# Two decoder layers in fp32 from one stream of loads: new order and places at the turn, w1 in seven groups, halves of exp

## The chip, the cores and the metric

The kernel runs on one core of a Trainium2 chip. The metric is the device time of one execution in microseconds. Everything is fp32.

## The reference

Two layers of decoding for 8 sequences, one token each. Each layer is attention over a cache of 4096 positions (32 query heads in 4 groups) and then a dense network of width 3584. Both layers use the same weights and the same caches.

```
def _A_ref(x, k_cache, v_cache, wq, wo):
    q = (x @ wq).reshape(B, Sq, Hq, Dh).transpose(0, 2, 1, 3)
    k = jnp.repeat(k_cache, rep, axis=1)
    v = jnp.repeat(v_cache, rep, axis=1)
    scores = jnp.einsum("bhqd,bhkd->bhqk", q, k) * (Dh ** -0.5)
    p = _softmax(scores, axis=-1)
    o = jnp.einsum("bhqk,bhkd->bhqd", p, v)
    return o.transpose(0, 2, 1, 3).reshape(B, Sq, Hq * Dh) @ wo

def _B_ref(x, w1, b1, w2, b2):
    h = _gelu(jnp.einsum("bsd,df->bsf", x, w1) + b1)
    return jnp.einsum("bsf,fd->bsd", h, w2) + b2

x = x + _A_ref(_layernorm(x), ...)
x = x + _B_ref(_layernorm(x), ...)
x = x + _A_ref(_layernorm(x), ...)
x = x + _B_ref(_layernorm(x), ...)
```

B = 8, D = 1024, Hq * Dh = 4096, F = 3584. Each cache is 64 MiB, wq and wo are 16 MiB each, w1 and w2 14 MiB each.

## The kernel before

**Memory.** Nearly all of SBUF is one tile, `arena`, of 52 units. A unit is 1024 columns of fp32 on 128 partitions, 512 KiB. A piece of K or V (one of 4 groups of heads, one half of the positions) is 1 MiB, two units; a batch has 8 pieces of K and 8 of V. All loads stand in one list, `stream`, in the order in which they are wanted: key, number of units, source and possible first units. `pump` (L214) takes from its head as long as the head's units are free, and issues the load on SP's queue. `release` (L226) frees a slot and pumps again. The queue is in order: a load that waits for its units holds all behind it. The order of PE's work is the order in which the program is written.

**Layer 0.** wq fills units 0 to 28 and goes on lying there through layer 0's attention, for layer 1 (`park`, L604, moves the rest of it aside). Units 48 to 52 hold the rows of scores and the turned probabilities (`arena.own`). Units 28 to 48 are a ring: `around` (L628) lists the caches' loads so that each begins where the last one ended, with at most 8 units in a load. For each batch `attention` (L572) goes through 8 pieces of K (`scores`, L479), then `probs` (L500: maximum over the positions, exp), `turn` (L512: eight transposes into `S`, two copies, and the total of exp by a matmul) and 8 pieces of V (`values`, L531). The result of each pair of V pieces is folded by DVE (L541, L543) and turned into a column of `oT` by `heads` (L548), one V piece later. In the last batch, 7, six pieces of K stay in units 36 to 48: layer 1 goes through the batches backwards and uses them first.

**Dense part of layer 0.** From the turn of batch 7 on, three blocks of 4 units, 28, 32 and 48, take wo (8 loads) and w1 (7 loads) in rotation. `expand` (L240) has w1 in three groups of 2048, 1024 and 512 columns (`GROUPS`). At the end of a group DVE takes it out (L264); at the next `flush` `hidden_unit` (L318) turns it, adds b1 and makes the gelu, into `hT`.

**The turn, `swap` (L382).** w2 comes in 4 columns of 28 tiles. Each column is three loads: a small one, "u", of 4 tiles (1 unit) that is given up after use, and 16 and 8 tiles (4 and 2 units) that stay for layer 1. For each column c PE does w2's products, DVE copies (L403), PE turns the result into x (L407), and then come the products of two tiles of wq (L417) with this new x, for the next layer's q. These free wq's units, into which the next columns of w2 and layer 1's first K and V are loaded. The small piece of column c+1 is used in `transient`, which is called between column c's copy and its turning, so ahead of column c's wq products. With the last column come the layernorm's moments and the square root (L465).

**Layer 1.** Attention over batches 7 to 0 in a ring over units 16 to 28 and 36 to 48, with at most 12 units in a load. Then wo in three loads (8, 12, 12 units), w1 in 12 and 4, 4 and 4, and 2, 1, 1 units, and the 4 small pieces of w2, the rest of which lies in the arena. `begin` runs w2's products for tiles 4 to 16 after the first half of w1's second group; the others come behind w1.

## Time and profile before

| | us |
|---|---|
| median of 3 runs | 899.94 (898.69 to 906.64) |
| the profiled execution | 903.69 |
| its span | 901.9 |
| PE busy | 556.9 |
| the load queue's packets, share of 16 DMA engines' span | 94.2% |
| read from HBM | 358.83 MB |

The span runs from the first to the last instruction of the program in one profiled execution; a run's time has some 1.8 us beside it. A page of the profile has each engine's busy time, the chain of waits that ended last, and groups of instructions by line (L488 is line 488 of the kernel) with what they waited for. PE is the matmul engine, PEld its weight loads, DVE and ACT the vector and the activation engine, SP the queue that issues loads. An fp32 matmul is two records. PEclk is the share of PE's full clock that was granted.

### The profile page before, as it was taken

To read this page: it belongs to the slowest core of one execution; us is meant where nothing else is said; L and a number is where in the kernel's file an instruction comes from. 1 tells how busy PE (TensorE), PEld (TensorE's weight loads), DVE (VectorE), ACT (ScalarE), POOL (GpSimd) and SP (SyncE) were. 2 spreads that over 40 slices of the span, in tenths; PEclk is the share of its full clock that TensorE was granted. 3 is DMA by queue.
4 is the path that set the end of the run, shared out by engine and by line. 5 is a ranking of instruction groups with operands and counts; after the bars stand their busy time and mean duration, and the time that the engine had idled before them with its cause. 6 is when DMAs were issued, how large, how long until landed. Compare 5 with 4: busy or idle time off the path is not lost.

```text
span 901.9 us, 9145 instructions
## 1 busy us (share of the span) xinstructions
PE 556.9 (62%) x4034; PEld 193.9 (22%) x4034; DVE 189.5 (21%) x616; ACT 50.1 (6%) x78; POOL 1.9 (0%) x12
## 2 busy tenths in 40 slices
PE   0767566665767576556568665666647567464477
PEld 0212122121212112222223221121202112122234
DVE  0013131212213131201211331322303122130011
ACT  0110000000000000000001100000000000000000
POOL 0000000000000000000000000000000000000000
PEclk9967778768667785878788986878868777787789
DMA  9999999999999998999996979999999999999990
GB/s 400 421 440 417 431 392 433 429 390 419 397 438 412 427 427 315 379 428 429 405 382 239 404 317 427 420 413 435 430 426 430 423 418 433 429 428 428 419 406 11
DMA packets 17895, 359.54 MB, mean 399 GB/s; under 512 B 1984, under 2 KB 2368, under 8 KB 3648
## 3 DMA queue, kind: packets, MB, share of 16 engines
q1 hardware_dynamic: 17712, 358.82, 94.2%
q8 instruction: 31, 0.51, 0.2%
q10 hardware_dynamic: 144, 0.15, 0.0%
q14 instruction: 8, 0.07, 0.0%
HBM read 358.83 MB, written 0.13 MB: 398 GB/s over the span
## 4 chain that ended last, share of the span: by engine, by line
DMA 48%; PE 37%; DVE 8%; ACT 3%; issue 2%; another core or an unknown queue 1%; SPq 0%; ACTq 0%; DVEq 0%
DMA arena<-in_k_dram 25%; PE sps L488 13%; PE o_ps L538 8%; DMA arena<-in_w_dram 7%; DMA arena<-in_wo_dram 6%; DMA arena<-in_v_dram 5%; DMA arena<-in_wq_dram 5%; PE sps L519 3%; PE acc L254 2%; ACT arena L509 2%; DVE arena L493 2%; PE y L371 2%; PE y L341 2%; PE acc L292 2%; PE sps L371 1%
## 5 line engine op out<-in xcount | busy, mean ns | idle before, releaser
L488 PE MATMUL sps<-arena,qz 128*32 128x512 f32 x1024 | 167.2, 805 | 118.1 <-DMA arena<-in_k_dram 109.5
L538 PE MATMUL o_ps<-arena 128*32 128x512 f32 x1024 | 162.5, 762 | 11.1 <-DMA arena<-in_v_dram 11.1
L488 PEld LDWEIGHTS sps<-arena,qz 128*32 128x32 f32 x1024 | 38.9, 139 | 242.1 <-issue 130.2
L493 DVE TENSOR_SCALAR_CACHE_REDUCE arena<-sps 128x512 f32<-128x512 f32 x32 | 22.1, 692 | 248.1 <-PE sps L488 248.1
L543 DVE SCALAR_TENSOR_TENSOR scr<-o_ps,bits,scr 128x128 f32<-128x128 f32 x192 | 67.4, 351 | 6.8
L341 PE MATMUL y<-arena,oxT 128*32 128x256 f32 x512 | 40.9, 481 | 39.8 <-DMA arena<-in_wo_dram 39.8
L519 PE MATMUL sps<-ident,arena 128*128 128x128 f32 x128 | 31.4, 391 | 38.6 <-DVE oxT L551 22.5
L538 PEld LDWEIGHTS o_ps<-arena 128*32 128x32 f32 x1024 | 31.4, 131 | 78.0 <-issue 62.4
L509 ACT ACTIVATE arena<-arena,bits 128x1024 f32<-128x1024 f32 x16 | 18.4, 1148 | 535.4 <-DVE scr L506 535.4
L254 PE MATMUL acc<-arena,oxT 128*32 128x512 f32 (+1 forms) x288 | 34.7, 616 | 17.0 <-DMA arena<-in_w_dram 16.4
L550 PE MATMUL sps<-bits,scr 128*128 128x8 f32 x128 | 25.8, 274 | 31.0 <-DVE scr L543 25.5
L541 DVE TENSOR_SCALAR scr<-o_ps,bits 128x128 f32<-128x128 f32 x64 | 22.5, 351 | 96.1 <-PE o_ps L538 96.1
L550 PEld LDWEIGHTS sps<-bits,scr 128*128 128x128 f32 x128 | 20.0, 197 | 86.3 <-DVE scr L543 73.6
L292 PE MATMUL acc<-arena,oxT 128*32 128x512 f32 (+1 forms) x250 | 34.4, 662 | 4.6 <-DMA arena<-in_wq_dram 4.3
L341 PEld LDWEIGHTS y<-arena,oxT 128*32 128x32 f32 x512 | 18.7, 134 | 61.6 <-DMA arena<-in_wo_dram 39.1
L519 PEld LDWEIGHTS sps<-ident,arena 128*128 128x128 f32 x128 | 20.2, 195 | 45.0 <-ACT arena L509 28.9
L371 PE MATMUL sps<-arena,oxT 128*32 128x256 f32 x224 | 17.8, 444 | 9.8 <-DMA arena<-in_w_dram 8.7
L502 PE MATMUL sps<-scr,bits 128*128 128x128 f32 x32 | 8.1, 337 | 21.3 <-DVE scr L498 21.3
L525 DVE COPY arena<-sps 128x512 f32<-128x512 f32 x16 | 11.1, 692 | 44.5 <-PE sps L519 44.5
L551 DVE TENSOR_TENSOR oxT<-sps,scr 128x8 f32<-128x8 f32 x64 | 11.0, 171 | 40.5 <-PE sps L550 40.5
L254 PEld LDWEIGHTS acc<-arena,oxT 128*32 128x32 f32 x288 | 11.0, 127 | 36.1 <-issue 18.9
L188 PE MATMUL sps<-ident,xb 128*128 128x128 f32 x12 | 3.1, 351 | 24.4 <-DMA xb<-in_x_dram 23.2
(106 smaller groups left out, 200.9 us busy)
## 6 DMA issues: line engine op xcount, KB each, us to landing
arena<-in_v_dram SPq DMA_DIRECT2D x16, 4096.0 KB, 17.6
arena<-in_k_dram SPq DMA_DIRECT2D x15, 4096.0 KB, 15.5
arena<-in_k_dram SPq DMA_DIRECT2D x16, 2048.0 KB, 16.7
arena<-in_v_dram SPq DMA_DIRECT2D x15, 2048.0 KB, 15.9
arena<-in_k_dram SPq DMA_DIRECT2D x5, 6144.0 KB, 18.6
arena<-in_v_dram SPq DMA_DIRECT2D x5, 6144.0 KB, 25.4
arena<-in_w_dram SPq DMA_DIRECT2D x14, 2048.0 KB, 12.5
arena<-in_wo_dram SPq DMA_DIRECT2D x8, 2048.0 KB, 11.5
```

Source lines behind the costliest of these rows:

```text
L254: nc.tensor.matmul(out_j, xnT[:, kt * XS:kt * XS + 32], src, start=(j not in begun), stop=(kt >= NT - (4 if split else 1)))
L292: nc.tensor.matmul(acc[u][32 * j:32 * j + 32, d0 - j * CH:d1 - j * CH], xnT[:, kt * XS:kt * XS + 32], ap[:, d0 - c0:d1 - c0], start=(kt == ...
L341: nc.tensor.matmul(y[32 * j:32 * j + 32, 0:Q4], lhs[:, n * B:n * B + 32], slot.ap[:, c + j * Q4:c + (j + 1) * Q4], start=(n == 0), stop=(n ...
L371: nc.tensor.matmul(y[32 * g:32 * g + 32], hT[:, kt * B:kt * B + 32], w2_at[c, kt], start=first, stop=(kt >= NFT - 4 if j is None else kt = ...
L488: nc.tensor.matmul(ps[32 * g:32 * g + 32, :], qz[:, c:c + 32], kt[:, g * CH:(g + 1) * CH], start=(j == 0), stop=(j == HKV - 1))
L493: nc.vector.tensor_scalar(st["row", b].ap[:, half * CH:(half + 1) * CH], ps, SCALE, None, op0=ALU.mult, op1=ALU.max, accum_out=st["mx", b] ...
L509: nc.scalar.activation(row, row, AF.Exp, bias=bias, scale=1.0, accum_out=ls)
L519: nc.tensor.transpose(pp[:, t * P:(t + 1) * P], row[:, c:c + P], ident)
L538: nc.tensor.matmul(o[32 * g:32 * g + 32, :], s[:, g], v[:, g * CH:(g + 1) * CH], start=(half == 0), stop=(half == NH - 1))
L541: nc.vector.tensor_scalar(r, o[:, 0:P], sel_t[:, 0:1], None, op0=ALU.mult)
L543: nc.vector.scalar_tensor_tensor(r, o[:, t * P:(t + 1) * P], sel_t[:, t:t + 1], r, op0=ALU.mult, op1=ALU.add)
L550: nc.tensor.matmul(po[:, 0:REP], r_s[j % 2], sel_h, start=True, stop=True)
```

## The change

In words:

- `swap`: `transient` is gone. Each column's three pieces of w2 are multiplied together, in the order `W2_ORDER` (the small one first or last), and the column's small piece is released there. The places of w2's loads are new.
- w1 is laid out in seven groups of 512 columns, each one block of 4 units. `expand` flushes ahead of each group. In layer 1 `grow` multiplies the w2 tiles of group u after w1's products of group u + 1.
- exp runs in two halves, each with its own total. `turn` transposes both halves, into two PSUM banks; DVE copies the first, ACT the second. The total's matmul is a new function, `totals`, after the second V piece. The second half of the scores has the bank `pt`.
- `heads` runs two tiles later than before, in the next batch if need be.
- Six pieces of batch 7's V are kept in place of six of its K.
- The ring functions are gone; each load's place is listed. wo in layer 1 comes in 4, 12, 8, 4, 2, 2 units, w1 in blocks of 4, the last one 2 and 2.
- `warm` runs a tanh right behind each square root.
- `bias_row` (the row of b2) is made during attention of layer 1 and added after the layernorm; in layer 0 it stays after w1's first group.

The diff, cut:

```diff
+W2_KTS = {"u": range(4), 0: range(4, 20), 1: range(20, NFT)}
+W2_ORDER = ("u", 0, 1), (0, 1, "u"), (0, 1, "u"), ("u", 0, 1)
+G = CH
+NGR = F // G
-GROUPS = 2048, 1024, 512
...
+    def warm():
+        nc.scalar.activation(sums["warm"], epst, AF.Tanh)
...
             nc.vector.reciprocal(rs, sd)
+            warm()
...
+        for u in range(NGR):
             acc = ps_o.tile([P, CH], F32, tag="o", name="acc")
+            kt = 0
+            flush()
             for i, slot in enumerate(tiles((name, u))):
+                for c in range(0, slot.cols, G):
+                    j = kt % 4
+                    nc.tensor.matmul(acc[32 * j:32 * j + 32, :], xnT[:, kt * XS:kt * XS + 32], slot.ap[:, c:c + G],
+                                     start=(kt < 4), stop=(kt >= NT - 4))
+                    kt += 1
                 release(slot)
                 flush()
+            if u in hooks:
+                hooks[u]()
+            nc.vector.tensor_scalar(row_s, acc, rs, None, op0=ALU.mult)
+            pending.append(lambda u=u: hidden_group(u, row_s))
...
+    def down_row(y, kts, cs=range(CB)):
         for kt in kts:
+            for c in cs:
+                nc.tensor.matmul(y[32 * c:32 * c + 32], hT[:, kt * B:kt * B + 32], w2_at[c, kt],
+                                 start=st["y0"][c], stop=(kt == NFT - 1))
...
     def swap():
+        flush()
         ys = small_ps("s")
-        transient(0)
-        flush()
...
         for c in range(CB):
-            for e, k0 in enumerate((UK, UK + 16)):
-                arrive(("w2", c, e), c, k0)
-            down(half(c), c, range(UK, NFT))
+            y = ys[:, c % 2 * Q4:(c % 2 + 1) * Q4]
+            kts = []
+            for kind in W2_ORDER[c]:
+                kts += arrive(c, kind)
+            down(y, c, kts)
+            release(held.pop(("w2u0", c)))
             ysb = row_s[:, c % 2 * Q4:(c % 2 + 1) * Q4]
-            nc.vector.tensor_copy(ysb, half(c))
-            if c + 1 < CB:
-                transient(c + 1)
+            nc.vector.tensor_copy(ysb, y)
...
-            st["ps", half] = small_ps("s")
+            st["ps", half] = small_ps(("s", "pt")[half])
...
-        nc.scalar.activation(row, row, AF.Exp, bias=bias, scale=1.0, accum_out=ls)
-        nc.vector.tensor_scalar(dl_s[b % 2], sel_x, ls, None, op0=ALU.mult)
+        for h in range(NH):
+            part = row[:, h * CH:(h + 1) * CH]
+            nc.scalar.activation(part, part, AF.Exp, bias=bias, scale=1.0, accum_out=ls[:, h:h + 1])
...
+    def turn(b):
...
+        for half in range(NH):
+            pp = small_ps(("pt", "s")[half])
...
+            if half == 0:
+                nc.vector.tensor_copy(dst, src)
+            else:
+                nc.scalar.activation(dst, src, AF.Copy)
...
+    def totals(b):
+        pl = small_ps("pt")
+        nc.tensor.matmul(pl[:, 0:HQ], ones, dl_s[b % 2], start=True, stop=True)
+        nc.vector.reciprocal(rl_s[b % 2], pl[:, 0:HQ])
+        st.pop(("row", b)).free()
...
+        def step():
+            for e in ready:
+                e[0] -= 1
+            while ready and ready[0][0] < 0:
+                heads(*ready.pop(0)[1:])
...
+                    if key[2:] == (0, NH - 1):
+                        totals(key[1])
+                step()
+                if key[0] == "v" and key[3] == NH - 1:
+                    ready.append([1, *key[1:3]])
...
-    kept = {("k", *k_at(last_b, r)) for r in range(n_kept)}
+    kept = {("v", *v_at(last_b, r)) for r in range(NR - n_kept, NR)}
...
+    cycle = [(((8, 32), (4, 40), (4, 44)), ((8, 28), (8, 36))), (((4, 44), (8, 28), (4, 36)), ((8, 40), (8, 28))),
+             (((8, 36), (4, 44), (4, 28)), ((8, 32), (8, 40))), (((8, 28), (4, 36), (4, 40)), ((4, 44), (8, 28), (4, 36))),
+             (((8, 40), (4, 28), (4, 32)), ((8, 36), (4, 44), (4, 28)))]
+    for n, b in enumerate(orders[0][:-1]):
+        batch(0, b, *cycle[n % 5])
+    batch(0, last_b, ((8, 36), (4, 44), (4, 28)), ((4, 32), (8, 36), (4, 44)))
...
+    for u in range(NGR):
+        weights(("i0", u), w1[0][:, u * NT * G:(u + 1) * NT * G], [4], blocks)
     i, j, k = LAST_BLOCKS
-    add(down_weights(0, ("u", 0, 1), 0), i + 3, j, i)
-    add(down_weights(1, ("u", 0, 1), 0), i + 2, k, i + 2)
-    add(down_weights(2, (0, 1, "u"), 0), 0, 4, 6)
-    add(down_weights(3, ("u", 0, 1), 0), 7, 8, 12)
+    down_weights(0, 0, i + 3, j, i)
+    down_weights(1, 0, k, i + 2, 0)
+    down_weights(2, 0, 2, 6, 1)
+    down_weights(3, 0, 0, 8, 12)
...
+    batch(1, last_b, ((4, 16), (4, 20), (4, 24), (4, 16)), ((4, 20),) if n_kept else ())
+    batch(1, last_b - 1, ((4, 24), (4, 16), (4, 20), (4, 36)), ((8, 40), (8, 16)))
...
+    weights(("o1",), wo[0], [4, 12, 8, 4, 2, 2], fixed(24, 36, 16, 24, 36, 38))
+    for u, (sizes, spots) in enumerate([([4], (at,)) for at in (40, 44, 16, 20, 24, 36)] + [([2, 2], (40, 42))]):
+        weights(("i1", u), w1[0][:, u * NT * G:(u + 1) * NT * G], sizes, fixed(*spots))
     for c in range(CB):
-        add(down_weights(c, ("u",), 1), 40 + c)
+        down_weights(c, 1, 44 + c)
...
+            groups = [range(GT * u, GT * (u + 1)) for u in range(NGR)]
+            expand("i1", rs, {u + 1: lambda u=u: grow(u) for u in range(1, NGR - 2)})
+            down_row(y[0], groups[NGR - 2][:2])
             flush()
+            down_row(y[0], groups[NGR - 2][2:])
             for c in range(CB):
+                arrive(c, "u")
+                down_row(y[0], groups[0], [c])
+            down_row(y[0], groups[NGR - 1])
             nc.vector.tensor_tensor(x_row, x_row, y[0], ALU.add)
```

The places in a pair such as (8, 32) are the number of units and the first unit; `LAST_BLOCKS` is now 28, 32, 48.

More of the change, by code (lines that the diff above doesn't have):

```diff
@@ L654, in lane, with cache @@
         return (layer, keys[0]), (kc if a == "k" else vc)[b][:, r * W:(r + m) * W]
-    def cache(layer, b, a, at, r=0):
+    def cache(layer, b, a, at):
+        r = 0
         while r < NR:
+            if layer == 1 and (a, *(k_at if a == "k" else v_at)(b, r)) in kept:
+                break
             n, starts = at(2 * (NR - r))
@@ L692, in decode_layers, with listed, batch @@
+    def listed(*spots):
+        spots = iter(spots)
+        return lambda left: next(spots)
+    def batch(layer, b, k_spots, v_spots):
+        for a, spots in (("k", k_spots), ("v", v_spots)):
+            stream.extend(cache(layer, b, a, listed(*((n, (at,)) for n, at in spots))))
     halves = lambda i: [[("q", kt, u) for kt in kts for u in range(2)] for kts in ((0, 1, 2, 3), (4, 5), (6,), ())][i]
     weights(("q0",), wq[0], [16, 8, 4, 4], fixed(0, 16, 24, 28), kept=halves)
-    ring = around(AREAS[0], 4, 8)
@@ L730, in decode_layers @@
         st["layer"] = layer
-        last = attention(orders[layer], kept if layer == 0 else (), {("turn", last_b): opened} if layer == 0 else {})
+        b2_row = spare[:, 0:Q4]
+        hooks = {("turn", last_b): opened} if layer == 0 else {
+            ("v", *v_at(last_b - 2, 0)): lambda: bias_row(b2_row, None, spare[:, Q4:Q4 + CH])}
+        last = attention(orders[layer], kept if layer == 0 else (), hooks)
         rsum = row_sums()
```

239 lines of the change are left out of this document (68 added, 171 removed).

## Prediction

> **What bounds the kernel now.** I read the page first, then a table of stretches with each stretch's granted clock and DMA rate, then the chain of waits inside the stretches that lose most.
>
> ```profile
> span 901.9 us, 9145 instructions
> ...
> PE 556.9 (62%) x4034; PEld 193.9 (22%) x4034; DVE 189.5 (21%) x616; ACT 50.1 (6%) x78; POOL 1.9 (0%) x12
> ...
> q1 hardware_dynamic: 17712, 358.82, 94.2%
> ```
>
> Then the stretches: start, end and length, busy time of each engine, granted clock, share of DMA time, GB/s.
>
> ```profile
> core 0: us, PE busy (x) PEld busy (x) DVE busy (x) ACT busy (x) POOL busy (x), PEclk, DMA share, GB/s
> 0.00:185.00 185.00, 104.88 (x646) 32.94 (x650) 35.13 (x112) 13.46 (x18) 1.57 (x11) 0.81 0.99 421
> 185.00:210.00 25.00, 18.29 (x108) 6.33 (x100) 7.73 (x26) 1.84 (x3) 0.00 (x0) 0.73 0.90 375
> 210.00:340.00 130.00, 83.17 (x484) 25.14 (x484) 31.59 (x102) 5.51 (x9) 0.00 (x0) 0.74 0.99 423
> 340.00:376.00 36.00, 22.64 (x120) 7.20 (x116) 9.14 (x30) 1.84 (x3) 0.00 (x0) 0.64 0.84 327
> 376.00:441.00 65.00, 37.58 (x394) 15.45 (x390) 5.12 (x15) 3.40 (x6) 0.00 (x0) 0.82 1.01 428
> 441.00:470.00 29.00, 20.40 (x208) 8.93 (x200) 5.01 (x19) 0.73 (x3) 0.31 (x1) 0.83 0.95 376
> 470.00:482.00 12.00, 7.49 (x41) 2.81 (x45) 0.17 (x1) 0.00 (x0) 0.00 (x0) 0.57 0.35 145
> 482.00:510.00 28.00, 23.87 (x255) 10.30 (x251) 8.30 (x27) 3.17 (x4) 0.00 (x0) 1.00 0.96 377
> 510.00:536.00 26.00, 17.92 (x118) 5.90 (x107) 9.06 (x29) 3.12 (x4) 0.00 (x0) 0.80 0.78 324
> 536.00:881.00 345.00, 204.96 (x1495) 70.41 (x1499) 74.23 (x240) 16.51 (x27) 0.00 (x0) 0.78 0.99 423
> 881.00:901.90 20.90, 15.75 (x202) 8.53 (x194) 4.00 (x15) 0.48 (x2) 0.00 (x0) 0.99 0.02 7
> ```
>
> One queue carries the loads and is busy 94.2% of the span; PE is busy 62%. So loads set the time wherever they run, and what can be won is the time in which they don't. The best long stretch (376 to 441) runs at 428 GB/s. I take that as the pace: 2 MiB (2.10 MB) is 4.90 us, the 512 KiB unit in which the kernel's places count 1.23 us. Each stretch loses its length times (1 - rate/428): 3.0 us to 185, 3.1 to 210, 1.5 to 340, 8.5 to 376, none to 441; then 3.5, 7.9, 3.3 and 6.3, together 21.0 us, to 536; 4.0 to 881. Behind the last load stand 20.9 us of PE work. The change doesn't alter the bytes: six kept pieces stay six, the kept part of w2 and wq stays the same. So the sum goes over three places: the turn between the layers (441 to 536), layer 0's last batch (340 to 376), and the tail.
>
> **The turn.** A row of the timeline (start, length; in brackets PE's idle time before it), then the longest pieces of the chain of waits behind it:
>
> ```profile
> 474.24 1.08 PE L371 MATMUL sps<-arena,oxT 128*32 128x256 f32 x8 [7.47 <-DMA arena<-in_w_dram]
> ```
>
> ```profile
> 477.18 5.82 PE acc L292 x30
> 482.99 2.85 PE sps L371 x45
> 488.20 3.44 PE acc L292 x30
> 491.64 2.83 PE sps L371 x45
> ```
>
> PE stands 7.47 us at 474 because the small w2 piece of column 2 (four tiles, `transient`) is queued on PE ahead of column 1's wq products, and it has not landed. Those wq products are what empties units 8 to 14 for column 3's loads, so the queue then stands too (145 GB/s in 470 to 482). The change puts each column's small piece into that column's own matmuls, behind the wq products of the column before; what PE waits for there is loaded before the places that those products empty. That hole goes.
>
> What is late next is the pace of a column itself. From 482.99 to 491.64 one column takes PE 8.65 us at clock 1.00: w2's matmuls, the copy, the turning, wq's products. It empties room for, and needs, seven units, 8.6 us of loads. These are as good as equal, so at full clock each of four columns may lose some tenths. The places agree: column 1's second piece (units 30, 31) waits for column 0's small piece to be read, which comes first in column 0's order; column 3's small piece (unit 0) waits for column 1's, the same way but last in its order, with three loads still ahead of it in SP's queue; columns 2 and 3 and the four K loads wait for wq products one column before their need. At half clock a column's wq products alone take 2.4 us more (5.82 against 3.44), w2's about as much: some 5 us a column. With no PE hole of several us I expect mostly full clock, as 482 to 510 had it. Column 0's large piece takes the place of the last w1 block but one, with 2.5 MiB queued in between instead of the 4 of three blocks in rotation: up to 2 us.
>
> All eight K pieces of batch 7 are now loaded instead of two, and its V is kept instead. This moves 6 MiB of loads ahead of the first scores in layer 1. They come through three blocks of 4 units that wq's last products empty, and are scored at 1.8 us a piece even near half clock (344.09 below: two pieces in 3.68) against 2.45 us of load, so PE keeps up; the V that is kept then needs no load, where in the trace of before the loads of 510 to 536 stood (324 GB/s) behind its values. I leave 3.5 us of the 21.0 (bounds 0 and 13: none, or half clock in two columns and a wait of 3 in the first batch). Gain 17.5 us.
>
> **Layer 0's last batch.** The longest pieces of the chain there:
>
> ```profile
> 344.09 3.68 PE sps L488 x16
> 347.80 0.71 DVE arena L493 x2
> 349.06 0.81 PE sps L502 x2
> 350.52 1.25 ACT arena L509 x2
> 352.26 1.10 PE sps L519 x4
> 354.03 1.13 PE sps L519 x4
> 355.18 0.70 DVE arena L525
> 356.57 5.32 PE o_ps L538 x24
> 361.91 7.75 DMA arena<-in_v_dram
> ```
>
> From the last score (347.77) to the first value take 8.8 us. K being kept in units 36 to 48, V has only units 28 to 36 until values free them, and comes in four loads of 1 MiB that each wait for values (361.91). With V kept, K's places 36 to 48 are free once scored, so all of V loads straight behind K, and two blocks of wo behind it into 28 and 32; the third needs 48 to 52, free when the last value is done. V's last load lands 9.8 us before the second wo block does, and V's last two pieces take PE 3.5 us at the rate of 356.57 (three in 5.32), so nothing stands. 8.5 us of loss become 1 (0 to 4). Gain 7.5.
>
> The shorter chain adds to that in each batch: halves of exp let the first four transposes start after 0.6 instead of 1.25 us, the second four go to another bank and no longer wait for the copy (0.67, from 353.36 to 354.03), and the copy's and the totals' time ahead of the first value (1.4, from 355.16 to 356.57) goes: some 2.5 us off 8.8. Heads, two tiles later, don't wait for DVE. A row of the waits: us in total, times, longest.
>
> ```profile
> PE sps L550 <- DVE scr L543: 25.5, 38, 0.8
> ```
>
> Under loads that are always running this is worth nothing; it counts where the ring stood, 185 to 210, where 3.1 us become 0.6: 2.5. The listed places walk through the same units in the same cyclic order as the old ring; only K's end now comes as a 2 MiB piece, so the last scores start with less to do. I count nothing for that, nor for the other stretches (3.0, 1.5, 4.0 stay). `warm` adds a table load of 1.28 us (874.37 below) on ACT behind each square root. At the turn the copy of q's second half is queued behind it, up to 1.3 us late (it lies in the turn's bounds); elsewhere ACT's next work comes some us later. The row of b2 for layer 1 is made in batch 5 of attention: two DVE products of 512 columns (0.67 each, as the eviction of 887.16 below) and the matmuls between, about 3 us of PE under running loads, so nothing, and 2 if the ring is full there. Layer 0's row of b2 now stands ahead of group 0's eviction and makes w1's first blocks 3 us late, within the 4.9 us that three blocks allow.
>
> **The tail.** The longest pieces of the chain, then one w1 block of layer 0 in the timeline.
>
> ```profile
> 874.37 1.28 ACT L329
> 876.44 5.39 PE y L371 x96
> 881.83 1.76 PE acc L254 x32
> 884.15 1.06 PE acc L254 x8
> 887.16 0.67 DVE scr L264
> 887.88 1.06 PE sps L273 x8
> 888.94 9.72 PE y L371 x128
> ```
>
> ```profile
> 416.31 1.92 PE L254 MATMUL acc<-arena,oxT 128*32 128x512 f32 x16 [1.18 <-DMA arena<-in_w_dram]
> ```
>
> Before, w1's first group is four blocks wide, so no w2 matmul can start until it is whole, turned and through tanh (876.44); by then loading is nearly over, and PE has all of w2 before it. After, a group is one block: 8 matmuls (1.92), four turning matmuls (1.06), and 16 w2 matmuls of the group before (a third of 5.39: 1.80), 4.8 us in all, beside 4.90 us of load; the eviction (0.67) lies beside the w2 matmuls. So at full clock PE is level with the loads. The last w1 block lands 4.9 us before the end of loading (2 MiB of small w2 pieces follow it). From there: 1.92, then the w2 matmuls of group 5 around the turning, about 3.1, which ends at the end of loading; then the small pieces and group 6's matmuls. 888.94 holds 64 matmuls; the first 32 at the rate of 876.44 are 3.6 us, so the other 32, the very ones that remain, 6.1. Then 3.2 us as now, from 898.66, where 888.94 ends, to the end of the span. 9.4 us; I take 10, bounds 9 and 15 (one block late). Gain 10.9.
>
> In the trace the clock is 0.99 in the busy tail and 0.57 in the stretch where PE stands; PE busy without gaps keeps it. [...]
>
> **Sum.** 17.5 + 7.5 + 2.5 + 10.9 = 38.4. 901.9 - 38.4 = 863.5 us of span. The profiled execution took 903.69, 1.8 more than its span, so 865.3 by its own measure; the median of the runs is 899.94, 3.75 below that execution. I predict 861.5.
>
> **Rivals.** *Half of the turn stays.* PE's column (8.65) against its loads (8.6) has no slack, and two columns at half clock, the first batch of layer 1 waiting for exp, and a tail at 15 give back 5 to 14: 867 to 877. For it: 470 to 482 ran at 0.57. Against: that clock followed PE's 7.47 us hole. 0.28.
>
> *A PE bound tail.* i1 at half clock throughout: 9.6 us a block against 4.9, five blocks late by 23, the end 6 longer: 891, within 1% of before. Against it: 0.99 in the tail of before. [...] 0.04.
>
> *The small pieces still hold the chain.* Units 30, 31 and 0 are reused by small pieces; if a hole of 8 us stays in another place, the time is 869. It lies inside the first rival and is counted there.
>
> *Slower.* The second half of the scores now shares a PSUM bank with heads, totals and the maximum's spread. If each batch's scores waited there until the ring's 10 MiB were full, every batch would stand. The gain of 38 is eaten at 2.6 us in each of 15 batches; 4 us in each give 921. For it: one such loss of 3.1 at 185 to 210. Against: heads run two tiles into the new batch, its bank is needed four tiles in. 0.05.
>
> **Numbers.** Forecast 0.59 (855 to 867), half the turn 0.28, tail 0.04, slower 0.05; 0.04 for better still: with none of the 10.6 us that I leave (3.5, 1, 0.6, 1.5, 4.0) and a tail of 9 it is 850. The range 849 to 879 leaves out somewhat over a tenth. One per cent, 9 us, is about what the runs (898.69 to 906.64) can tell from no change. Faster by more: 0.59 + 0.28 + 0.04 = 0.91; within: 0.04; slower: 0.05.
>
> **What would show it.** Right: no stretch of the turn under 350 GB/s, no PE wait over 3 us for a small w2 piece; no V load of 1 MiB in layer 0; w2 matmuls of layer 1 beginning some 22 us before loading ends, and 9 to 15 us between the last load and the end. Wrong: clock near 0.5 in the turn with wq products at 5.8 us, loads standing behind w2's places, or PE still at w1 blocks when the last load has landed.

## The result and the profile after

The changed kernel takes 863.33 us (median of 4 runs, 859.75 to 867.36) against 901.62 for the kernel before on the same chip (4 runs, 898.69 to 906.64). The ratio is 0.957, with a 95% interval of 0.951 to 0.964. 861.5 was predicted, with a range of 849 to 879. The profiled execution took 861.56, its span 859.8.

The page of the changed kernel: the loads' queue is now busy 98.1% of the span instead of 94.2%, and the bytes are the same.

```profile
span 859.8 us, 9370 instructions
...
PE 541.6 (63%) x4054; PEld 193.9 (23%) x4054; DVE 202.1 (24%) x689; ACT 56.8 (7%) x122; POOL 1.7 (0%) x12
...
q1 hardware_dynamic: 19152, 358.82, 98.1%
```

The changed kernel by stretches, cut at the places that answer to those of before: first the batches of layer 0, the stretch where the ring stood, the last batch (332 to 365), wo and w1, then the turn (426 to 518) in four parts, layer 1, and the tail. Columns as before.

```profile
core 0: us, PE busy (x) PEld busy (x) DVE busy (x) ACT busy (x) POOL busy (x), PEclk, DMA share, GB/s
0.00:178.00 178.00, 99.27 (x652) 31.66 (x652) 34.83 (x116) 14.50 (x25) 1.57 (x11) 0.84 0.99 425
178.00:203.00 25.00, 15.03 (x101) 5.35 (x97) 7.36 (x25) 2.12 (x5) 0.00 (x0) 0.86 1.02 436
203.00:332.00 129.00, 78.08 (x471) 24.45 (x472) 30.69 (x105) 6.35 (x15) 0.00 (x0) 0.75 1.00 429
332.00:365.00 33.00, 23.22 (x164) 7.88 (x158) 9.80 (x34) 2.12 (x5) 0.00 (x0) 0.79 1.01 428
365.00:426.00 61.00, 37.79 (x368) 16.52 (x368) 10.63 (x37) 4.46 (x10) 0.00 (x0) 0.83 1.00 416
426.00:455.00 29.00, 22.96 (x239) 11.21 (x243) 6.64 (x26) 0.69 (x3) 0.15 (x1) 0.94 0.96 389
455.00:466.00 11.00, 9.28 (x113) 3.80 (x106) 1.82 (x3) 2.31 (x2) 0.00 (x0) 1.00 1.01 419
466.00:493.00 27.00, 18.65 (x173) 6.89 (x165) 6.46 (x24) 2.24 (x4) 0.00 (x0) 0.93 1.00 414
493.00:518.00 25.00, 21.47 (x156) 7.28 (x148) 10.22 (x34) 2.12 (x5) 0.00 (x0) 0.80 0.94 392
518.00:849.60 331.60, 208.84 (x1576) 75.04 (x1580) 83.25 (x287) 19.96 (x48) 0.00 (x0) 0.77 1.00 426
849.60:859.80 10.20, 7.04 (x80) 3.79 (x74) 0.42 (x1) 0.00 (x0) 0.00 (x0) 1.00 0.04 14
```

Read with the prediction's rule (a stretch loses its length times 1 - rate/428), most of the loss is where the prediction looked for it, and about two thirds of it is gone (62.0 us before, 19.8 after):

| us lost | before | predicted | measured |
|---|---|---|---|
| layer 0 up to its last batch | 7.6 | 5.1 | 0.5 |
| layer 0's last batch | 8.5 | 1 | 0 |
| wo and w1 of layer 0 | 0 | 0 | 1.7 |
| the turn | 21.0 | 3.5 | 5.9 |
| layer 1 behind it | 4.0 | 4.0 | 1.5 |
| work behind the last load | 20.9 | 10 | 10.2 |

The columns' differences from before are 38.4 predicted and 42.2 measured, for a span that became 42.1 shorter. One row of the table of waits for PE in 426 to 466 of the changed kernel (us in total, times, longest) shows that the hole at the small piece of column 2, 7.47 us before, is gone:

```profile
PE sps L366 <- DMA arena<-in_w_dram: 2.6, 3, 1.7
```

The end of the chain of waits of the changed kernel (start, length, what): w1's last blocks (L255), w2's products of the group before (L372), turnings (L313), then all that is left.

```profile
839.56 1.92 PE acc L255 x16
841.49 1.73 PE sps L372 x32
843.21 0.99 PE sps L313 x8
844.20 1.85 PE acc L255 x16
...
849.45 7.20 PE sps L372 x80
```

A block costs 4.6 us of PE (1.85 + 1.73 + 0.99) against 4.9 of load, as the prediction had it (4.8), and the first of w2's products of layer 1 run at 827, 22 us before loading ends.

### The profile page after: what moved, and what is told of

The parts are those of the page before. It is cut to its first block, busy times and chain, and to the rows that moved or that the text cites. A ratio compares the mean times of both kernels' runs of the same rounds, so it can differ in the third digit from the quotient of the medians.

```text
span 859.8 us, 9370 instructions
## 1 busy us (share of the span) xinstructions
PE 541.6 (63%) x4054; PEld 193.9 (23%) x4054; DVE 202.1 (24%) x689; ACT 56.8 (7%) x122; POOL 1.7 (0%) x12
## 3 DMA queue, kind: packets, MB, share of 16 engines
q1 hardware_dynamic: 19152, 358.82, 98.1%
## 4 chain that ended last, share of the span: by engine, by line
DMA 69%; PE 26%; DVE 2%; issue 1%; ACT 1%; another core or an unknown queue 1%; SPq 0%; ACTq 0%; DVEq 0%
DMA arena<-in_v_dram 26%; DMA arena<-in_k_dram 24%; DMA arena<-in_wo_dram 10%; PE o_ps L539 8%; PE sps L483 8%; DMA arena<-in_w_dram 6%; DMA arena<-in_wq_dram 5%; PE acc L255 2%; PE y L335 2%; PE sps L372 1%; PE sps L366 1%; PE acc L284 1%; PE sps L313 1%; PE sps L515 1%
## 5 line engine op out<-in xcount | busy, mean ns | idle before, releaser
L539 PE MATMUL o_ps<-arena 128*32 128x512 f32 x1024 | 166.9, 779 | 85.2 <-DMA arena<-in_v_dram 85.2
L483 PE MATMUL sps<-arena,qz 128*32 128x512 f32 x1024 | 151.2, 734 | 97.1 <-DMA arena<-in_k_dram 96.5
L483 PEld LDWEIGHTS sps<-arena,qz 128*32 128x32 f32 x1024 | 33.2, 126 | 180.6 <-DMA arena<-in_k_dram 96.3
L539 PEld LDWEIGHTS o_ps<-arena 128*32 128x32 f32 x1024 | 33.7, 131 | 149.3 <-issue 115.7
L506 ACT ACTIVATE arena<-arena,bits 128x512 f32<-128x512 f32 x32 | 22.8, 714 | 529.2 <-DVE scr L501 529.2
L515 PE MATMUL sps<-ident,arena 128*128 128x128 f32 x128 | 28.5, 380 | 24.7 <-ACT arena L506 24.4
L551 PEld LDWEIGHTS sps<-bits,scr 128*128 128x128 f32 x128 | 21.5, 211 | 67.3 <-issue 37.5
L284 PE MATMUL acc<-arena,oxT 128*32 128x512 f32 (+1 forms) x250 | 32.1, 622 | 4.8 <-DMA arena<-in_wq_dram 4.6
L255 PE MATMUL acc<-arena,oxT 128*32 128x512 f32 x224 | 30.6, 669 | 0.7 <-DMA arena<-in_w_dram 0.7
L551 PE MATMUL sps<-bits,scr 128*128 128x8 f32 x128 | 27.3, 286 | 0.0
L515 PEld LDWEIGHTS sps<-ident,arena 128*128 128x128 f32 x128 | 20.0, 188 | 30.1 <-ACT arena L506 30.1
L313 PE MATMUL sps<-bits,scr 128*128 128x8 f32 x112 | 15.6, 266 | 8.2 <-DVE scr L263 8.2
L313 PEld LDWEIGHTS sps<-bits,scr 128*128 128x128 f32 x112 | 14.4, 201 | 20.0 <-DVE scr L263 18.4
## 6 DMA issues: line engine op xcount, KB each, us to landing
arena<-in_v_dram SPq DMA_DIRECT2D x11, 2048.0 KB, 20.6
```

The lines of the kernel that those rows point to most:

```text
L255: nc.tensor.matmul(acc[32 * j:32 * j + 32, :], xnT[:, kt * XS:kt * XS + 32], slot.ap[:, c:c + G], start=(kt < 4), stop=(kt >= NT - 4))
L284: nc.tensor.matmul(acc[u][32 * j:32 * j + 32, d0 - j * CH:d1 - j * CH], xnT[:, kt * XS:kt * XS + 32], ap[:, d0 - c0:d1 - c0], start=(kt == ...
L313: nc.tensor.matmul(pt[:, i * B:(i + 1) * B], row[:, i * P:(i + 1) * P], bsel, start=True, stop=True)
L483: nc.tensor.matmul(ps[32 * g:32 * g + 32, :], qz[:, c:c + 32], kt[:, g * CH:(g + 1) * CH], start=(j == 0), stop=(j == HKV - 1))
L506: nc.scalar.activation(part, part, AF.Exp, bias=bias, scale=1.0, accum_out=ls[:, h:h + 1])
L515: nc.tensor.transpose(pp[:, t * P:(t + 1) * P], row[:, c:c + P], ident)
```

## The experiments

Each is an edit of the changed kernel, one of the kernel before. Medians in us; "span" and "last load" (when the last load landed) are those of the profiled execution. The kernel before had medians of 904.1 to 904.8 beside them. "And first products twice" and "turning behind" are further edits of "tail by tiles". Not taken out by themselves were `warm`, the place of `bias_row` and the new places in layer 1; what each of these is worth is not shown.

| | median (runs) | ratio to before, 95% | span | last load |
|---|---|---|---|---|
| K kept | 866.23 (864.71 to 874.51) | 0.959, 0.952 to 0.965 | 865.9 | 855.1 |
| small pieces ahead again | 871.77 (871.10 to 872.91) | 0.963, 0.960 to 0.966 | 869.7 | 857.8 |
| w2 behind w1 | 873.54 (864.50 to 875.93) | 0.963, 0.957 to 0.969 | 874.1 | 852.3 |
| old chain | 868.61 (864.24 to 869.28) | 0.958, 0.955 to 0.962 | 866.9 | 855.8 |
| old ring | 865.05 (858.41 to 866.69) | 0.955, 0.951 to 0.960 | 856.6 | 846.3 |
| old ring, old chain | 871.12 (869.73 to 872.32) | 0.963, 0.960 to 0.967 | 870.5 | 859.4 |
| before, new order alone | 893.83 (891.86 to 900.09) | 0.989, 0.985 to 0.993 | 892.0 | 867.9 |
| tail by tiles, `warm` later | 862.11 (858.82 to 868.25) | 0.954, 0.949 to 0.959 | 861.8 | 852.5 |
| tail by tiles | 860.70 (859.39 to 865.63) | 0.952, 0.948 to 0.956 | 859.6 | 851.8 |
| and first products twice | 864.00 (859.79 to 870.99) | 0.956, 0.952 to 0.960 | 858.0 | 849.7 |
| the changed kernel again | 865.46 (861.58 to 867.61) | 0.956, 0.953 to 0.960 | 865.8 | 856.0 |
| tail by tiles, turning behind | 860.71 (858.95 to 867.84) | 0.953, 0.950 to 0.956 | 862.7 | 850.4 |

Below, the loss of a load is the time by which it lands later than 1.225 us per unit (4.90 us per 2 MiB) behind the load before it, from the trace's list of transfers. Not all of it comes from PE: each of the fourteen traces has three to six loads that were issued 6 us or more before the load ahead of them landed, and still lost over 0.4 us each, 4.0 to 6.8 us together (4.3 in the changed kernel). What holds these up is not known.

### The order of w2's small pieces

The small piece of column c+1 is multiplied ahead of column c's wq products again, with the places of before:

```diff
+        transient(0)
...
             nc.vector.tensor_copy(ysb, y)
+            if c + 1 < CB:
+                transient(c + 1)
...
```

> The changed kernel with each column's small w2 piece multiplied ahead of the wq products of the column before, and in the places it had before. My theory: PE stands 5 to 8 us for one small piece, the loads stand 6 to 10 us behind it in the column loop; 870 to 876 us. Rival, the hole came from the full ring and the long chain before it and not from the order: 863 to 867 us, PE's longest wait for a small piece under 3 us.

The hole came back, in PE's timeline and then in the loads (the kernel with this edit):

```profile
458.25 1.08 PE L366 MATMUL sps<-arena,oxT 128*32 128x256 f32 x8 [6.81 <-DMA arena<-in_w_dram]
```

```profile
461.00:466.00 5.00, 5.00 (x29) 1.42 (x25) 0.00 (x0) 0.00 (x0) 0.00 (x0) 0.50 0.01 3
```

PE stands 6.81 us, runs the wq products at half clock, and meanwhile the queue moves 3 GB/s. Column 3's large load loses 8.0 us and the first K load behind it 3.0. By the ratios, 0.963 against 0.957 of the changed kernel (0.956 when it was run again), the order and its places are worth some 5 to 6 us of the median; the interval of 0.963 overlaps with that of 0.957 and meets that of 0.956 at 0.960, so the size is loose, but the hole in the trace is plain.

The opposite, the kernel before with this order and the places that follow from it, and nothing else:

> The kernel before with one part alone: w2's small pieces multiplied with their own column, behind the wq products of the column before, and the places that follow. My theory: the PE wait of 7.5 us and the 8 us for which the loads stood behind it go, the rest of the turn's 21 us (the start of the columns, the first batch of layer 1 with K kept, the last batch of layer 0) stays: 8 to 11 us off, 891 to 895 us. Rival, the order carries the whole turn: 16 us or more off, under 888. Second rival, without V kept the loads stand elsewhere: less than 4 us off.

```profile
340.00:376.00 36.00, 20.60 (x134) 7.63 (x134) 9.30 (x31) 1.84 (x3) 0.00 (x0) 0.76 0.92 361
441.00:470.00 29.00, 24.76 (x266) 11.75 (x262) 5.65 (x19) 2.79 (x4) 0.31 (x1) 0.82 0.93 373
470.00:482.00 12.00, 9.58 (x111) 4.19 (x115) 1.48 (x5) 0.00 (x0) 0.00 (x0) 1.00 1.01 424
482.00:510.00 28.00, 19.45 (x144) 7.20 (x140) 8.53 (x31) 3.98 (x6) 0.00 (x0) 0.88 0.91 379
510.00:536.00 26.00, 13.55 (x104) 3.52 (x100) 6.83 (x21) 0.00 (x0) 0.00 (x0) 0.80 0.87 363
```

470 to 482 runs at 424 GB/s (145 before), and the median is 10.7 us lower, as the theory had it. But the turn still loses 11 us by the rate rule, most of it behind 482, where layer 1's first batch still has its V to load: the order takes the hole, the rest of the turn needs the other parts. The 10.7 is not the turn alone: in the profiled execution the turn lost 10 us less, the last batch of layer 0 2.9 less, and the work behind the last load was 3.5 longer (24.2 us from its landing to the end, against 20.7).

### V or K of batch 7 kept

Six pieces of K kept instead of V, with places to match:

```diff
-    kept = {("v", *v_at(last_b, r)) for r in range(NR - n_kept, NR)}
+    kept = {("k", *k_at(last_b, r)) for r in range(n_kept)}
...
```

> The changed kernel (863.3 us) with six pieces of batch 7's K kept again in place of its V, and the places that follow from it. My theory, three separate places that add up: layer 0's last batch loses 7 to 8 us again, because its V has only 8 units to come through, and layer 1's first batch another 1 to 5; 871 to 876 us, the tail and the column loop as in the changed kernel. Rival, the shorter chain from the scores to the values is what removed the loss and V's place is worth nothing: 863 to 866 us, no stretch around the last batch under 400 GB/s.

The last batch of layer 0 with K kept, a stretch and two places of the chain: last scores (L483), transposes (L515), first values (L539), then a V load that had to wait for values.

```profile
336.00:372.00 36.00, 22.08 (x140) 7.95 (x144) 9.01 (x31) 2.12 (x5) 0.00 (x0) 0.74 0.93 372
```

```profile
337.57 1.97 PE sps L483 x16
...
342.90 1.97 PE sps L515 x8
344.87 2.55 PE o_ps L539 x16
...
348.81 9.20 DMA arena<-in_v_dram
```

The waiting V load is there, but the stretch loses 36 x (1 - 372/428) = 4.7 us, not the 7 to 8 that I had set on it, nor nothing, as the rival had it. By the list of transfers the V loads lose only 0.9 of this; 3.4 lie at the first two wo loads behind them, issued at 357.66 and 360.10, when values had freed their units. The median, 866.23, came out below the 871 to 876 expected, and its ratio of 0.959 can't be told from the changed kernel's; the cost of keeping K is read from this one trace. In the chain 5.3 us lie between the last score (339.54) and the first value, where the kernel before had 8.8. Whether the shorter chain takes a part of the loss here is not shown, since the kernel before with only the new order, which has the old chain, lost 5.6 (361 GB/s above) and the kernel before 8.5. With V kept nothing is lost with the new chain, and 0.8 us by the rate rule with the old one (418 GB/s in 334 to 368 of the next experiment). Keeping V is enough by itself.

### The shorter chain and the listed places

One kernel has exp whole, both transposes in one bank, the totals in `turn` and heads one tile later, as before; one has the ring of before for batches 0 to 6 of layer 0; one has both.

```diff
...
-        for h in range(NH):
-            part = row[:, h * CH:(h + 1) * CH]
-            nc.scalar.activation(part, part, AF.Exp, bias=bias, scale=1.0, accum_out=ls[:, h:h + 1])
+        nc.scalar.activation(row, row, AF.Exp, bias=bias, scale=1.0, accum_out=ls[:, 0:1])
...
```

```diff
...
-    for n, b in enumerate(orders[0][:-1]):
-        batch(0, b, *cycle[n % 5])
+    ring = around(((28, 48),), 4, 8)
+    for b in orders[0][:-1]:
+        stream.extend(cache(0, b, "k", ring))
+        stream.extend(cache(0, b, "v", ring))
```

> The changed kernel with exp in one piece, the turning, the totals and the heads as before and the scores in one bank. My theory: under running loads the chain is worth nothing except where the ring stood; 0 to 4 us, 863 to 867, losses of 1 to 3 us at single batches of layer 0. Rival, the shorter chain carries the gain at the ring, at the last batch and at the turn: 870 to 878 us, and the last batch of layer 0 loses 3 us or more.

> The changed kernel with the old ring's sizes and places for batches 0 to 6 of layer 0 (K's end often in one block of 8 units). The old chain under the listed places lost nothing in layer 0's batches, so the chain is not what closed those losses by itself. If the listed places closed them, the old ring under the new chain loses 3 to 7 us in layer 0's batches: 866 to 871 us. If either of the two is enough, it loses under 2 us: 863 to 866.

> The changed kernel with the old ring in layer 0 and the old chain from scores to values. If either alone is enough to close the losses, they are back only here: 6 to 8 us in batches 0 to 6 of layer 0, 872 to 878 us. If the places do it all, this equals the run with the old ring alone plus 0 to 3 us. If neither does, under 2 us of loss there and 866 to 869 us.

The same stretch, 150 to 340, in four kernels: before; old ring and old chain; old chain with listed places; old ring with the new chain.

```profile
150.00:340.00 190.00, 124.37 (x708) 38.21 (x712) 47.20 (x151) 7.95 (x13) 0.00 (x0) 0.74 0.98 417
```

```profile
150.00:340.00 190.00, 125.54 (x712) 37.59 (x712) 46.85 (x151) 7.35 (x12) 0.00 (x0) 0.73 0.98 417
```

```profile
150.00:340.00 190.00, 122.10 (x729) 35.59 (x728) 47.56 (x152) 7.35 (x12) 0.00 (x0) 0.77 1.00 429
```

```profile
150.00:340.00 190.00, 116.35 (x732) 36.23 (x730) 46.98 (x160) 9.06 (x21) 0.00 (x0) 0.80 1.00 430
```

417, 417, 429 and 430 GB/s: the ring's loss is 190 x (1 - 417/428) = 4.9 us with both old (6 to 8 had been expected), and either of the two alone removes it. They are not additive. With both old nearly all of it lies at two loads, the first 4 MiB of K of a batch (2.9 us at 212.1, 1.8 at 253.1), each issued only about 1 us before the load ahead of it landed. My reading is that each of the two parts gets such a load issued earlier, by time or by room; what it is in the listed places that gives the room (the pieces' sizes or where they begin) was not taken apart.

The medians fit: 871.12 with both old (872 to 878 expected), 868.61 and 865.05 with one. The old chain alone lies above the 863 to 867 expected for it, but its ratio, 0.958, is that of the changed kernel within the intervals, and 3.7 us of what its trace loses lie at w1's loads in layer 0, which the edit does not touch.

### w1 in seven groups, w2 between them

Layer 1's products of w2 all behind w1, with the seven groups left as they are:

```diff
-            expand("i1", rs, {u + 1: lambda u=u: grow(u) for u in range(1, NGR - 2)})
-            down_row(y[0], groups[NGR - 2][:2])
+            expand("i1", rs)
             flush()
-            down_row(y[0], groups[NGR - 2][2:])
+            for u in range(1, NGR - 1):
+                grow(u)
```

> The changed kernel with layer 1's w2 matmuls of groups 1 to 5 all behind w1's last block instead of between the blocks. My theory: five groups of 16 matmuls at 1.8 us each, one of which was behind the loads' end anyway, move behind the last load: tail 10.3 + 7 = 17.5 us, 870 us. Rival from the clock, PE idles between w1's blocks, drops to half rate and keeps it: tail 25 to 30 us, 878 to 883. Second rival, w1 in small blocks alone made the tail short: 863 to 865.

The stretch of w1's last blocks of that kernel, and the longest piece of its tail:

```profile
833.00:853.60 20.60, 18.00 (x88) 7.47 (x80) 5.97 (x23) 0.87 (x4) 0.00 (x0) 0.50 0.84 346
```

```profile
856.11 14.90 PE sps L372 x224
```

21.8 us lie behind the last load, between the two theories' numbers. Of the 11.6 us more than in the changed kernel, 7.7 are the moved records (224 in 14.90 us against 80 in 7.20); the rest is that PE was still at w1 when the last load had landed (852.32) and came to w2 only at 856.11. From 833 to 853.6 PE had half clock throughout, and a w1 block took 6.3 us on PE. That is how the prediction's rival of a tail bound by PE comes about. In the changed kernel w2's products lie between the blocks, in the time of the evictions, and its clock is 0.99 from 820 to 849.6. The loss does not come in each execution: one of the four took 864.50, no more than the changed kernel, and no trace shows what was different in it.

### The tail by tiles

In layer 1 the last small pieces are multiplied tile by tile over the four columns, instead of column by column. The four columns write different quarters of the output's partitions.

```diff
             for c in range(CB):
                 arrive(c, "u")
-                down_row(y[0], groups[0], [c])
+            down_row(y[0], groups[0])
```

First together with `warm` moved behind the copy of q's second half at the turn, and then alone:

> The changed kernel with two further edits: the last 16 w2 matmuls of the small pieces go tile by tile over the four columns instead of column by column (four at a time fit side by side in the array, 0.43 us a row as the matmuls of the other groups: 1.8 instead of 3.7 us), and the tanh behind the turn's square root comes after the copy of q's second half. My theory: tail 10.3 to 8.4 us, and up to 1.5 us in the loads behind the first scores of layer 1; 860 to 862 us. Rival, the small pieces' landing sets the end and not PE: tail unchanged, 862 to 864.

> The changed kernel with one edit: in layer 1 the last small pieces of w2 are multiplied tile by tile over all four columns, once all four have landed, instead of piece by piece; nothing else. Theory (neighbouring matmuls that write different quarters of the output run beside each other; four of one column in a row write the same quarter): the work behind the last load falls from 10.3 us to 8.4 to 9.3, and the median by 0.9 to 1.9 from that of the changed kernel, 863.3 before. Rival: pieces multiplied early hide what their form costs, and nothing is left to win: no difference.

```profile
852.43 6.25 PE sps L372 x80
```

```profile
851.93 4.57 PE sps L372 x80
```

The same 80 records as the 7.20 us of the changed kernel; 32 of them, those of the small pieces, are in another order. In the first kernel 3.4 us of them ran at half clock; in the second none did, and 7.9 us lie between the last load (851.76) and the end, 2.3 fewer than in the changed kernel and more of a gain than the 0.9 to 1.9 expected. `warm`'s new place won nothing that shows: the first K load that waits for layer 1's scores lost 1.8 us, 1.6 and 2.3 in the two traces of the changed kernel. Over six runs each on one chip the second kernel's mean is 861.36, the changed kernel's 865.15. The difference is 3.8 with an interval of 0.9 to 6.7 (from the twelve times by Student's t); the traces account for about 2.3 of it. This version is faster than the changed kernel.

### Looking for the source of the spread

The changed kernel itself, run again:

> The changed kernel as it is, on the chip of the two runs above, so that all are compared with the same runs of the kernel before: 863 us, ratio 0.957; work behind the last load 10.3 us.

A profiled span of 865.8 instead of 859.8, from the same program; the work behind the last load is 9.8 us. The w1 blocks of layer 0 in this execution, as a stretch and as a chain:

```profile
411.00:421.00 10.00, 9.13 (x43) 4.15 (x46) 3.01 (x13) 0.46 (x2) 0.00 (x0) 0.50 0.77 298
```

```profile
412.27 3.62 PE acc L255 x16
...
415.92 0.76 DVE scr L263
...
416.72 1.87 PE sps L313 x8
418.59 3.23 PE acc L255 x16
```

At half clock a block is 3.62 + 0.76 + 1.87 = 6.25 us on PE, which waits for the eviction (L263), against 4.9 of load. From 411 on the half clock lasts 10.2 us here, and 6.8 from 410.7 on in the first profile; here the first block, too, ran at half clock (3.62 us of PE from 403.95 on, against 1.90). w1's loads lose 4.7 us here, 0.8 there.

Two attempts to take that away, both on top of the tail by tiles. One computes the first four products of each w1 block of layer 0 twice, so that PE is busier:

```diff
+                    if kt < 4 and st["layer"] == 0:
+                        nc.tensor.matmul(acc[32 * j:32 * j + 32, :], xnT[:, kt * XS:kt * XS + 32], slot.ap[:, c:c + G],
+                                         start=True, stop=True)
```

> The edit of the run above, and in layer 0 the first four products of each of the seven w1 blocks are computed twice (the first result is overwritten), so that PE has some 3.9 us of work in a block of 4.9 us instead of 3.0. Theory A (the granted clock in the w1 blocks falls because PE idles there, and at half clock a block takes 5.9 to 6.4 us of PE against 4.9 of load, so the loads stand): no or shorter half clock windows between the start of the w1 blocks and the turn (10 us in the run before this, 6.8 in the changed kernel), loss of the w1 blocks' loads 0 to 0.5 us instead of 0.8 to 3.4. Theory B (the windows come whatever PE does): blocks at half clock then take 8 us, and the loss there grows to 6 us or more.

```profile
408.60:412.00 3.40, 3.40 (x20) 0.77 (x12) 0.65 (x4) 0.23 (x1) 0.00 (x0) 0.50 0.97 414
```

Half clock lasts 3.4 us and w1's loads lose 0.7, close to the first theory; the second, with 6 us or more, falls. But the kernel beside it without the doubling also had half clock for only 3.4 us behind its first block (411.2 to 414.6). It lost 2.9, and its first block, before the doubling could matter, had run at half clock where this one's had not. So one profile each doesn't show that the doubling shortened anything. And column 0's loads now lose 2.4 us. The median is no better, 864.00 against 860.70.

The other lets each block's turning run behind the next block's products, so that no eviction stands in PE's row:

```diff
-            flush()
+            if u == 0 or st["layer"] == 1:
+                flush()
```

> The kernel with the last small pieces of w2 tile by tile, and one more edit: in layer 0 each w1 block's turning comes behind the next block's products instead of ahead of them, so that PE no longer stands for the eviction (0.76 us a block) and gives a block's units back 1.06 to 1.9 us earlier. Theory (at half clock the block's row on PE of 3.6 + 0.76 + 1.87 = 6.25 us is longer than its load of 4.9, and the gap in it keeps the clock down): the row without the gap is 5.5 us at half clock, the half clock window ends within 3.4 to 7 us, and w1's loads lose 0 to 1.2 us instead of 0.8 to 5.0; median 0 to 3 us below 860.7, and a smaller spread of the runs. Rival (these windows are not what sets the spread): w1's loads lose nothing here either, but median and spread stay as they are, the loss coming back at column 0 of the turn, whose large pieces go into the units of w1's last blocks and need h whole, now 1 us later: 861 to 863.

```profile
433.88 1.00 PE sps L314 x8
...
436.28 0.67 DVE scr L264
...
437.09 1.85 PE sps L314 x8
438.94 5.55 PE sps L367 x56
```

w1's loads lose nothing now, although 10.2 us of the blocks ran at half clock. But the last two turnings come late, and column 0 of w2 starts behind them, at 438.94; without this edit it had started at 439.14. Column 0's loads lose 2.1 us. This is where the rival had put the loss, but not shown to be its cause: the large piece that lost was issued at 428.48, before the late turnings. By column 2's second piece the two kernels are level (it lands at 460.8 here, 460.7 without the edit): what w1 saved is gone. The median is the same, 860.71, and the spread no smaller, as the rival had it.

The profiled span of 862.7 is still 3.1 us longer than without this edit, and all of that lies behind the last load, in layer 1, which the edit leaves alone: 12.3 us instead of 7.9. From 816 to 830 w1's first blocks ran at half clock, PE came to the last w2 products 3.0 us behind the last load, and these took 6.2 us instead of 4.6. So w2's products between the blocks don't rule out half clock in the blocks ahead of them. What sets the spread is not settled: the half clock in w1's blocks of either layer is one part (4.7 against 0.8 us, 12.3 against 7.9), the loads that lose time without waiting for PE may be another.

## Why the prediction came out right, and where not

The time was right within 1.8 us, partly because two errors cancel: the span came out 3.7 us below the 863.5 of the sum, and the median lies 3.5 above the profiled span where the prediction set it 2.0 below. Within the span, too, errors cancel: layer 0's batches, its last batch and layer 1 lost 4.6, 1 and 2.5 us less than predicted, the turn and w1 in layer 0 2.4 and 1.7 more. That the median fell so near was luck.

*The turn: mechanism right, size short.* The hole went with the order of the small pieces, shown both ways. 5.9 us stayed instead of 3.5, within the bounds of 0 to 13. They lie at the loads that wait for column 0's products (389 GB/s in 426 to 455) and at the first batch (392 GB/s in 493 to 518), the two places that the prediction had named; column 0's own large piece, set at up to 2 us, lost nothing. In the first batch PE waited 4.5 us for a K load and then had half clock from 490 to 500. No wait for a w2 piece is above 1.7 us. The sign "no stretch of the turn under 350 GB/s" holds for the four stretches of the table, of 11 to 29 us, but depends on their length: cut by 5 us, 445 to 450 runs at 283 and 500 to 505 at 239 GB/s.

*Layer 0's last batch: right.* 0 of 8.5 us, predicted 1. All of it was credited to keeping V, and V kept does suffice. Whether the new chain alone would have taken a part is not shown.

*The ring: the step that failed.* "The listed places walk through the same units in the same cyclic order as the old ring; only K's end now comes as a 2 MiB piece [...]. I count nothing for that." The old chain with the listed places runs at 429 GB/s, without loss, so they are enough without the chain, and the chain's 2.5 us are not its own. The term was also too small: it was booked for 185 to 210 alone, while all of layer 0 up to its last batch lost 7.6 us and now loses 0.5. In the trace of before the first K load of a batch had lost 2.3 us at 134.0 and 1.1 at 254.9 as well as 2.7 at 214.7.

*w1 in layer 0: missed.* "3 us late, within the 4.9 us that three blocks allow" looked at the row of b2 alone, and at full clock. The new blocks have a gap for the eviction and 4.9 us of load each; at half clock they take 6.25 us and are longer than their loads. This took 0.8 us in one profiled execution of the changed kernel and 4.7 in the other.

*The tail: right in the profiled execution.* 10.2 against 10, with the same parts. A clock at half up to w1's last block came only where the w2 products were taken out from between them (0.50 from 833 to 853.6). But in another execution, with the turning behind, the first w1 blocks of layer 1 ran at half clock (3.64 and 3.57 us of products against 1.85), and the tail took 12.3 us where 7.9 had been measured. What made the clock fall there was not shown.

*Slower by a shared bank: no.* The stretches from 178 to 332 run at 429 GB/s or more, and the old chain with one bank is not faster.

One sum of the prediction is off: its first rival gives back 5 to 14 us, which from 861.5 is 866.5 to 875.5, not 867 to 877.

## What to carry to other kernels

When one queue of loads sets the time, book a loss to the place where the queue stands, and ask which other edit would remove the same loss: two parts that each give the chain slack don't add up. Put a product that waits for a load behind the products that free the places for later loads. A gain on one load in front of a serial PE chain may be worth only what the next load that waits for the same chain lets through, as the turning behind the next block showed up to column 2.

## What the runs showed of the hardware

Busy work does not always raise PE's clock at once. Five neighbouring stretches of 3.4 us, a length of which the half clock in w1's blocks of layer 0 lasted one, two or three, from the second run of the changed kernel:

```profile
407.60:411.00 3.40, 1.42 (x11) 0.47 (x8) 1.77 (x3) 0.00 (x0) 0.00 (x0) 1.00 0.95 337
411.00:414.40 3.40, 3.40 (x19) 1.78 (x22) 1.13 (x6) 0.23 (x1) 0.00 (x0) 0.50 0.89 376
414.40:417.80 3.40, 2.53 (x13) 1.08 (x6) 0.75 (x1) 0.00 (x0) 0.00 (x0) 0.50 0.48 120
417.80:421.20 3.40, 3.40 (x20) 1.30 (x20) 1.13 (x6) 0.23 (x1) 0.00 (x0) 0.50 0.92 390
421.20:424.60 3.40, 2.52 (x28) 1.33 (x24) 1.50 (x5) 0.00 (x0) 0.00 (x0) 0.99 0.90 306
```

The clock falls behind a stretch in which PE was busy for 1.42 us, and rises behind a full one, but not behind the first full one. In the trace of before no fall of the clock stands behind 3.4 us with more than 1.79 us of PE work (167.81 to 171.22), in the first profile of the changed kernel none behind more than 2.22 (407.29 to 410.70): in these two traces PE busy without gaps kept the clock. In the kernel with w2 behind w1, half clock went on for 20.6 us (833 to 853.6) at 87% busy. The first full stretch above holds 2.2 us of w1's products and 1.2 of turnings (L313, matmuls of eight columns), the second 2.7 and 0.7. In layer 0 of both traces of the changed kernel, and of tail by tiles and its two edits, w1's products took 2.7 us or more in seven further stretches of 3.4 us at half clock behind which the clock rose, and 1.8 or less in those behind which it did not; in layer 1 of the kernel with w2 behind w1, 2.5 us did not raise it. That the short turnings count less is a guess that no run tested. Which blocks the half clock met differed between executions of the same program.

The 80 records of w2's last products took 7.20 us when the 32 of the small pieces wrote the same quarter of the output's partitions four matmuls running, and 4.57 when these, too, went round the quarters, at clock 1.00 both times. By the trace of the changed kernel one such record is 379 ns long, and the 32 of a group between the w1 blocks take 1.93 us together (827.19), so neighbouring ones overlap there.

The tanh behind each square root moved the table load to itself (L189, four times) from the exp (L509, twice) or the gelu's tanh (L329, twice) that came next; either kernel has nine such loads of 1.28 us. At the turn the load now stands ahead of ACT's copy of q's second half (477.20), as the prediction had said. ACT at the first exp of layer 1, before, and at the tanh and the first exp after:

```profile
514.24 1.28 ACT L509 ACT_TABLE_LOAD   x1 [12.61 <-DVE scr L506]
515.53 1.15 ACT L509 ACTIVATE arena<-arena,bits 128x1024 f32<-128x1024 f32 x1
```

```profile
475.71 1.28 ACT L189 ACT_TABLE_LOAD   x1
...
496.81 0.72 ACT L506 ACTIVATE arena<-arena,bits 128x512 f32<-128x512 f32 x1 [19.12 <-DVE scr L501]
```

Behind the tanh, the exp of 496.81 has no load of its own; the one of 515.53 before, behind a square root whose load was at 484.28, had 1.28 us.
